# Routed attention into a SwiGLU layer: another order for the first head pair, zero matmuls between its assignments, and new steps for the preparation of pairs 2 to 6

## The chip, the cores and the metric

The kernel runs on one core of one Trainium2 chip. The metric is the device time of one execution in microseconds (us); the time of the kernel before is the median of three runs. Engine names are those of the profile: PE is TensorE's matmuls, PEld its weight loads, DVE is VectorE, ACT is ScalarE, POOL is GpSimd, SP is SyncE, which here only issues DMAs.

## The reference

Attention by clusters and then a feed-forward layer. Every query and key is assigned to the nearest of 16 centroids of its head, and a query attends only to keys of its own cluster.

```python
# q, k, v: 4 batches x 8 heads x 768 tokens x 64; centroids: 8 heads x 16 x 64
q_assign = argmax(einsum('bhsd,hcd->bhsc', q_n, c_n))      # k_assign alike
mask = q_assign[:, :, :, None] == k_assign[:, :, None, :]
scores = where(mask, matmul(q, k^T) / sqrt(64), -1e9)
attn = softmax(scores);  x = attn @ v                      # x: 3072 tokens x 512
xn = x / rms(x) * rms_g
out = (silu(xn @ w_gate) * (xn @ w_val)) @ w_out           # d_ff 1536
```

## The kernel before

Heads go in pairs: pair `pi` holds two heads of one batch, and there are 16 pairs, four to a batch. One head of one batch is a *slot* (32 of them). The mask is made part of the scores' matmul: for each head a tile `aug` of 80 rows holds 64 rows of q (or k) and 16 rows that are a one-hot code of the cluster, so that one matmul with a depth of 80 gives score and mask together. There are three sets of `aug` tiles, so pair 4 uses the set of pair 1.

**Steps.** The main loop goes through steps; a slot has 9 steps (`NCH`), and `at(step, fn)` hangs a piece of other work on a step. In the first 96 steps a score tile is *wide*: every third step four matmuls (L375) fill 128x1536 of PSUM, in three banks, and one ACT instruction takes the exponential of it (L378, `pT<-scw`). There are 32 such wide chunks, and chunk k belongs to steps 3(k-1) to 3k-1. Two wide tiles exist, so the matmuls of chunk k wait for the exponential of chunk k-2. In steps 2 to 7 of a slot `pv_group` multiplies the slot before with its values (L389), and in step 8 `pv_norm` normalises it on DVE (L398, L399). From step 96 on (`FFN0`) the feed-forward matmuls of the finished batch (L477, L510) run between narrower score tiles.

**Preparing a pair** (`prep_parts`) has 13 pieces, hung on steps in this order: T0 to T3 turn q and k of the two heads (three transposes on PE into one PSUM tile, L209, and a copy of 128x384 out of it, L213 on DVE or L215 on ACT); CAST writes the 64 rows of `aug` on POOL (L220); SP multiplies with the centroids (L233); TR, MX, CMP, SCL and BACK make the one-hot code on DVE (L240, L245, L250, L256, L261); PLACE sends its rows into `aug` by four DMAs (L272); CASTV turns v into bf16 on POOL (L225). The tiles of T0 to T3 and of SP all come from `ps_t`, a pool of one PSUM bank, so each waits until the one before has been read.

**Every engine works in the written order** (`manual_schedule`): nothing is reordered, and an instruction that waits holds all that are behind it on its engine.

**The first pair** can't be prepared ahead, and has code of its own: it makes the one-hot code by tokens (`assign0`, `pick0`) and brings it into rows by a matmul with an identity (`rows0`, `rows1`). `keep_warm` issues matmuls of zeros that nothing reads. A pool `ps_first` of six PSUM banks serves all of this, and is closed before the two wide tiles take its banks; the first turn of pair 1 is also in it. Where `t_tile` is called before that, it takes `ps_first`.

Of the kernel before, what the change touches and what calls it, by code (L numbers as in the profile page):

```python
# [8 lines left out]
F32 = mybir.dt.float32  # L9
# [4 lines left out]
PSUM = bass.MemoryType.PSUM  # L14
# [5 lines left out]
def kernel(  # L20
# [12 lines left out]
    nc = tc.nc  # L33
    B, H, S, D = q.shape
    NC = centroids.shape[1]
# [28 lines left out]


    first = ExitStack()
    ps_first = first.enter_context(tc.tile_pool(name="ps_first", bufs=6, space=PSUM))
    wide = ExitStack()
    WCH = 3
    late = {}  # L70
# [62 lines left out]

    def keep_warm(n, w_ps=None):
        if w_ps is None:
            w_ps = ps_first.tile([P, CH], F32, name="w_ps", tag="f")
        for _ in range(n):
            nc.tensor.matmul(w_ps, lhsT=zeros[:, 0:P], rhs=zeros, start=True, stop=True)  # L138
        return w_ps
# [19 lines left out]
    def put_centroids():  # L159
        c_ps = ps_t.tile([P, P], F32, name="c_ps", tag="t")  # L160
        nc.tensor.transpose(c_ps, c2[:, :, :].rearrange("p a d -> p (a d)"), ident_f)
        c_pv.append(c_ps[:, :].rearrange("p (h c) -> p h c", c=NC))
        nc.vector.tensor_copy(cbd[0:D, 0:2, :, 0], c_pv[0][0:D, 0:2, :])
        nc.scalar.copy(cbd[D:P, 0:2, :, 1], c_pv[0][D:P, 0:2, :])

    def rest_of_centroids():
        nc.vector.tensor_copy(cbd[0:D, 2:, :, 0], c_pv[0][0:D, 2:, :])
        nc.vector.tensor_copy(cbd[D:P, 2:, :, 1], c_pv[0][D:P, 2:, :])
# [17 lines left out]


    def t_tile(name):
        pool, tag = ps_t, "t"
        if "wide" not in late:  # L190
            pool, tag = ps_first, "f"
        return pool.tile([P, HS], F32, name=name, tag=tag)

    def prep_parts(pi):
        st = pi % NSET
# [3 lines left out]
        def t_group(g):  # L199
            a, side = divmod(g, 2)  # L200
            if qk32[0] is None:
                qk32[0] = prep.tile([P, 4, HS], F32, name="qk32", tag="qk32", bufs=3)
            if pi == 1 and g in (1, 3):
                tp = ps_pv.tile([P, HS], F32, name="tp", tag="acc")
            else:
                tp = t_tile("tp")
            src = loads[pi, side]
            for i in range(TH):
                nc.tensor.transpose(tp[:, i * P:(i + 1) * P], src[:, a, i * P:(i + 1) * P], ident_f)  # L209
            dst = qk32[0][:, g, :]  # L210
            on_dve = g > 0 if pi == 1 else pi < 7 or g % 2
            if on_dve:
                nc.vector.tensor_copy(dst, tp)  # L213
            else:
                nc.scalar.copy(dst, tp)  # L215
# [63 lines left out]
    as0 = {}  # L279
    oh0 = {}  # L280

    def turn0(g):
        tp = ps_first.tile([P, HS], F32, name="tp", tag="f")
        a, side = divmod(g, 2)
        for i in range(TH):
            nc.tensor.transpose(tp[:, i * P:(i + 1) * P], loads[0, side][:, a, i * P:(i + 1) * P], ident_f)  # L286
        if a:
            nc.vector.tensor_copy(qk0[:, g, :], tp)
        else:
            nc.scalar.copy(qk0[:, g, :], tp)  # L290

    def cast0(a):
        for side in range(2):
            for par in range(2):
                src = qk0[par * D:(par + 1) * D, 2 * a + side, :]
                dst = aug[0][a][0:D, side, par * HS:(par + 1) * HS]
                if a:
                    nc.gpsimd.tensor_copy(dst, src)
                else:
                    nc.scalar.copy(dst, src)  # L300

    def assign0(a, side):
        if a == 0:
            as0[a, side] = ps_first.tile([P, TH * 2 * NC], F32, name="as0", tag="f")
            dst = as0[a, side]
        else:
            if side == 0:
                as0[a] = ps_pv.tile([P, 2, TH * 2 * NC], F32, name="as1", tag="acc")
            dst = as0[a][:, side, :]
        for i in range(TH):  # L310
            nc.tensor.matmul(dst[:, i * 2 * NC:(i + 1) * 2 * NC], lhsT=qk0[:, 2 * a + side, i * P:(i + 1) * P],  # L311
                             rhs=cbd[:, a, :, :].rearrange("p c r -> p (c r)"), start=True, stop=True)

    def pick0(a, sides, src):
        n = len(sides) * TH
        view = src.rearrange("p (n c r) -> p n r c", c=NC, r=2)
        mx = small.tile([P, n, 2], F32, name="mx0", tag="mx0")
        nc.vector.tensor_reduce(mx, view, axis=AX, op=ALU.max)
        if a not in oh0:
            oh0[a] = const.tile([P, 2, TH * 2 * NC], BF16, name=f"oh0{a}")  # L320
        for j, side in enumerate(sides):
            nc.vector.tensor_tensor(oh0[a][:, side, :].rearrange("p (n c r) -> p n r c", c=NC, r=2),
                                    view[:, j * TH:(j + 1) * TH], mx[:, j * TH:(j + 1) * TH, :].unsqueeze(3)
                                    .to_broadcast([P, TH, 2, NC]), op=ALU.is_ge if side else ALU.is_lt)

    def rows0(side):
        o_ps = ps_first.tile([P, HS], F32, name="o_ps", tag="f")
        ov = oh0[0][:, side, :].rearrange("p (n c r) -> p n r c", c=NC, r=2)
        for i in range(TH):
            for r in range(2):  # L330
                nc.tensor.matmul(o_ps[32 * r:32 * r + NC, i * P:(i + 1) * P], lhsT=ov[:, i, r, :],
                                 rhs=(ident_n, ident_b)[side], start=True, stop=True, tile_position=(0, 32 * r))
        for r in range(2):
            dst = aug[0][0][D:KA, side, r * HS:(r + 1) * HS]
            if r:
                nc.vector.tensor_copy(dst, o_ps[32 * r:32 * r + NC, :])
            else:
                nc.scalar.copy(dst, o_ps[32 * r:32 * r + NC, :])

    def rows1():  # L340
        o_ps = ps_t.tile([P, HS], F32, name="o_ps", tag="t")
        for i in range(TH):
            for side in range(2):
                nc.tensor.matmul(o_ps[32 * side:32 * side + 32, i * P:(i + 1) * P],
                                 lhsT=oh0[1][:, side, i * 2 * NC:(i + 1) * 2 * NC],
                                 rhs=(ident_n, ident_b)[side], start=True, stop=True, tile_position=(0, 32 * side))
        o_sb = const.tile([64, HS], BF16, name="o_sb")
        nc.vector.tensor_copy(o_sb, o_ps[0:64, :])
        for side in range(2):
            nc.sync.dma_start(out=aug[0][1][D:KA, side, :].rearrange("c (r n) -> c r n", r=2),  # L350
                              in_=o_sb[32 * side:32 * side + 2 * NC, :])
# [192 lines left out]

    T0, T1, T2, T3, CAST, SP, TR, MX, CMP, SCL, BACK, PLACE, CASTV = range(13)
    p0, p1, p2, p3 = (prep_parts(pi) for pi in range(4))
    turn_w = keep_warm(7)
    turn0(0)
    turn0(1)
    turn0(2)  # L550
    put_centroids()
    turn0(3)
    keep_warm(2, turn_w)
    assign0(0, 0)
    assign0(0, 1)
    pick0(0, (0,), as0[0, 0][:, :])
    cast0(0)
    pick0(0, (1,), as0[0, 1][:, :])
    rows0(0)
    assign0(1, 0)  # L560
    rows0(1)
    assign0(1, 1)
    rest_of_centroids()
    pick0(1, (0, 1), as0[1][:, :, :].rearrange("p a n -> p (a n)"))
    cast0(1)
    p1[T0]()
    first.close()
    late["wide"] = wide.enter_context(tc.tile_pool(name="ps_wide", bufs=2, space=PSUM,
                                                 reuse_waits="tile"))
# [4 lines left out]
    for i, step in ((T1, 0), (T2, 3), (T3, 4), (CAST, 5), (SP, 6), (TR, 6), (MX, 7), (CMP, 8), (SCL, 9), (BACK, 10),  # L574
                    (PLACE, 10), (CASTV, 11)):
        at(step, p1[i])
    for i, step in ((T0, 10), (T1, 14), (T2, 16), (T3, 19), (CAST, 20), (SP, 21), (TR, 21), (MX, 22), (CMP, 23), (SCL, 24),
                    (BACK, 25), (PLACE, 25), (CASTV, 26)):
        at(step, p2[i])
    for i, step in ((T0, 24), (T1, 27), (T2, 29), (T3, 31), (SP, 33), (CAST, 33), (TR, 34), (MX, 35), (CMP, 36), (SCL, 37),  # L580
                    (BACK, 38), (PLACE, 38), (CASTV, 40)):
        at(step, p3[i])
    for pi in range(2, 4):
        at(10, lambda pi=pi: load_part(pi, 2))
# [21 lines left out]
    for pi in range(4, B * NP):  # L606
        base = 2 * NCH * (pi - 2) + {7: 14, 8: 10, 9: 4}.get(pi, 0)
        steps = (-11, -8, -5, -2, 0, 0, 2, 3, 4, 5, 6, 7, 10)
        if pi == 4:
            steps = (0, 2, 4, 7, 9, 9, 10, 12, 13, 14, 15, 16, 18)  # L610
        elif pi == 5:
            steps = (-6, -3, -1, 2, 4, 4, 5, 6, 7, 8, 9, 10, 12)
        elif pi == 6:
            steps = (-11, -8, -5, -2, 0, 0, 2, 3, 4, 4, 5, 6, 7)
        elif pi > 6:
            steps = (-8, -6, -4, -2, 0, 0, 2, 3, 4, 5, 6, 6, 10)
        for fn, step in zip(prep_parts(pi), steps):
            at(base + step, fn)
        if pi < B * NP - 3:
            at({6: 100, 7: 118}.get(pi, base + 12), lambda pi=pi: load_pair(pi + 3))  # L620
# [62 lines left out]
```

## Time and profile before

| | |
|---|---|
| time, median of three runs (lowest, highest) | 349.26 us (348.62, 350.96) |
| the profiled execution's own time; its span | 351.38 us; 349.6 us |
| PE busy, share of the span | 336.0 us, 96% |
| DVE busy, ACT busy, POOL busy | 223.4, 226.3 and 90.4 us |
| wide exponentials (L378, 128x1536) | 32, of 1456 ns in the mean |
| idle time of ACT before them | 13.4 us |
| narrow exponentials (L378, 128x512) | 192, of 598 ns |
| copies of T0 to T3 on DVE (L213, 128x384) | 41, of 551 ns |

The page lists busy time, then the span in 40 slices of 8.7 us with a digit for the busy tenths and one for the TensorE clock that was granted, then the costliest groups of instructions with the idle time of their engine before them and what ended it. A busy engine isn't an engine at its peak[...]. Other views answer for a stretch of time: the timeline (start, duration, engine, line, tiles, idle time before and what ended it), the chain that ended last, and busy time by windows.

### The profile page before, as it was taken

To read this page: it belongs to the slowest core of one execution; us is meant where nothing else is said; L and a number is where in the kernel's file an instruction comes from. 1 tells how busy PE (TensorE), PEld (TensorE's weight loads), DVE (VectorE), ACT (ScalarE), POOL (GpSimd) and SP (SyncE) were. 2 spreads that over 40 slices of the span, in tenths; PEclk is the share of its full clock that TensorE was granted. 3 is DMA by queue.
4 is the path that set the end of the run, shared out by engine and by line. 5 is a ranking of instruction groups with operands and counts; after the bars stand their busy time and mean duration, and the time that the engine had idled before them with its cause. 6 is when DMAs were issued, how large, how long until landed. Compare 5 with 4: busy or idle time off the path is not lost.

```text
span 349.6 us, 7568 instructions
## 1 busy us (share of the span) xinstructions
PE 336.0 (96%) x2948; PEld 208.8 (60%) x2980; DVE 223.4 (64%) x469; ACT 226.3 (65%) x391; POOL 90.4 (26%) x125
## 2 busy tenths in 40 slices
PE   8998888999999999999999999999999999999996
PEld 5655565676676566565656656566666655555554
DVE  3476678869676667776656468785545577756550
ACT  4487777998786677776767668687777434232322
POOL 4265689309531303141030214120000001000000
PEclk9699999999999999999999999999999999999999
DMA  7165899952944405145141001212000012200012
GB/s 260 64 217 173 194 278 222 261 163 50 248 90 139 158 29 182 53 36 194 33 146 43 2 36 39 47 57 62 33 1 32 30 50 58 77 30 30 33 60 90
DMA packets 36739, 34.94 MB, mean 100 GB/s; under 512 B 13520, under 2 KB 33632, under 8 KB 36704
## 3 DMA queue, kind: packets, MB, share of 16 engines
q1 hardware_dynamic: 30496, 29.44, 26.7%
q0 software_dynamic: 5920, 4.79, 9.1%
q8 instruction: 23, 0.38, 0.4%
q10 hardware_dynamic: 288, 0.23, 0.2%
q14 instruction: 12, 0.10, 0.1%
HBM read 28.61 MB, written 6.29 MB: 100 GB/s over the span
## 4 chain that ended last, share of the span: by engine, by line
PE 87%; DVE 5%; ACT 2%; DMA 2%; issue 1%; POOLq 0%; POOL 0%; DVEq 0%; ACTq 0%
PE gp L477 17%; PE vp L477 17%; PE dp L510 17%; PE sc L375 12%; PE acc L389 8%; PE tp L209 6%; PE scw L375 3%; PE sp L233 3%; DMA aug<-ohT 2%; ACT pT L378 2%; PE w_ps L138 1%; DVE qk L213 1%; PE as L311 1%; PE tp L286 1%; DVE ohT L261 1%
## 5 line engine op out<-in xcount | busy, mean ns | idle before, releaser
L378 ACT ACTIVATE pT<-sc 128x512 bf16<-128x512 f32 x192 | 113.7, 598 | 44.5 <-PE sc L375 44.1
L486 DVE SCALAR_TENSOR_TENSOR uu<-th,gp 128x384 f32<-128x384 f32 x96 | 53.0, 552 | 66.3 <-ACT th L482 66.2
L477 PE MATMUL vp<-xnT,wv 128*128 128x384 bf16 x384 | 78.1, 325 | 0.2 <-DVE gvT L492 0.2
L477 PE MATMUL gp<-xnT,wg 128*128 128x384 bf16 x384 | 78.1, 325 | 0.1
L389 PEld LDWEIGHTS <-pT 128*128 128x128 bf16 x1152 | 57.5, 97 | 30.2 <-issue 2.8
L482 ACT ACTIVATE th<-gp 128x384 f32<-128x384 f32 x96 | 47.2, 492 | 43.3 <-PE gp L477 40.6
L375 PE MATMUL sc<-aug 80*128 80x512 bf16 (+1 forms) x256 | 73.0, 327 | 0.0
L510 PE MATMUL dp<-wo,gvT 128*128 128x512 bf16 (+1 forms) x268 | 71.2, 369 | 1.6
L220 POOL CAST aug<-qk 64x768 bf16<-64x768 f32 x60 | 51.8, 863 | 64.7 <-DVE qk L213 46.9
L389 PE MATMUL acc<-vbf,pT 128*128 128x65 bf16 x1152 | 63.8, 194 | 1.5 <-DVE x L399 0.7
L492 DVE TENSOR_TENSOR gvT<-uu,vp 128x384 bf16<-128x384 f32 x96 | 52.6, 548 | 5.8 <-PE vp L477 0.8
L477 PEld LDWEIGHTS <-wg 128*128 128x128 bf16 x384 | 37.2, 97 | 30.1 <-issue 0.6
L378 ACT ACTIVATE pT<-scw 128x1536 bf16<-128x1536 f32 x32 | 45.7, 1456 | 13.4 <-PE scw L375 12.9
L477 PEld LDWEIGHTS <-wv 128*128 128x128 bf16 x384 | 37.1, 97 | 18.6 <-issue 0.5
L375 PEld LDWEIGHTS <-aug 80*128 80x128 bf16 x384 | 33.8, 99 | 17.3 <-issue 8.1
L510 PEld LDWEIGHTS <-gvT 128*128 128x128 bf16 x300 | 29.2, 98 | 24.3
L213 DVE COPY qk<-tp 128x384 f32<-128x384 f32 x41 | 22.5, 551 | 16.5 <-PE tp L209 16.4
L375 PE MATMUL scw<-aug 80*128 80x512 bf16 (+1 forms) x128 | 27.3, 337 | 0.7 <-ACT qk L215 0.6
L443 DVE SCALAR_TENSOR_TENSOR xn<-x,ir,g_b 128x512 bf16<-128x512 bf16 x24 | 20.3, 862 | 5.3 <-POOL ir L435 4.3
L225 POOL CAST vbf<-v_in 128x768 bf16<-128x768 f32 x16 | 13.5, 844 | 34.7 <-issue 34.3
L209 PE MATMUL tp<-ident_f,k_in 128*128 128x128 f32 x90 | 16.2, 291 | 2.7 <-DVE qk L213 2.7
L399 DVE TENSOR_TENSOR x<-acc,inv 128x384 bf16<-128x384 f32 x32 | 17.8, 557 | 1.1
(84 smaller groups left out, 206.6 us busy)
## 6 DMA issues: line engine op xcount, KB each, us to landing
v_in<-in_v_dram SPq DMA_DIRECT2D x16, 384.0 KB, 4.6
out_dram<-ob SPq DMA_DIRECT2D x23, 256.0 KB, 2.0
q_in<-in_q_dram SPq DMA_DIRECT2D x15, 384.0 KB, 4.6
k_in<-in_k_dram SPq DMA_DIRECT2D x15, 384.0 KB, 4.3
wg<-in_moe_w_gate_dram POOLq DMA_DIRECT2D x4, 384.0 KB, 8.1
wv<-in_moe_w_val_dram POOLq DMA_DIRECT2D x4, 384.0 KB, 7.9
wo<-in_moe_w_out_dram POOLq DMA_DIRECT2D x4, 384.0 KB, 7.3
aug<-ohT SPq DMA_DIRECT2D x57, 24.0 KB, 2.3
```

Of the source, the lines that this page charges most:

```text
L209: nc.tensor.transpose(tp[:, i * P:(i + 1) * P], src[:, a, i * P:(i + 1) * P], ident_f)
L213: nc.vector.tensor_copy(dst, tp)
L220: nc.gpsimd.tensor_copy(aug[st][a][0:D, :, par * HS:(par + 1) * HS], qk32[0][par * D:(par + 1) * D, 2 * a:2 * a + 2, :])
L375: nc.tensor.matmul(sc[:, o:o + n], lhsT=ag[:, 1, kc * P:(kc + 1) * P], rhs=ag[:, 0, qo:qo + n], start=True, stop=True)
L378: nc.scalar.activation(pts[slot][:, j * CH:(j + nch) * CH], sc[:, :nch * CH], ACT.Exp, scale=scale)
L389: nc.tensor.matmul(acc[:, TORD[g], :], lhsT=pts[slot][:, kc * S + g * P:kc * S + (g + 1) * P], rhs=vb[:, a, TORD[kc], :], start=(kc == 0), ...
L443: nc.vector.scalar_tensor_tensor(st["xn"][:, tl, :], x_t[b][:, t, :], st["ir", m][:, tl:tl + 1], g_b, op0=ALU.mult, op1=ALU.mult)
L477: nc.tensor.matmul(pt[:, :HS], lhsT=w[:, dc, fc * P:(fc + 1) * P], rhs=xnT[b, m][:, :, dc, :], start=(dc == 0), stop=(dc == DC - 1))
L482: nc.scalar.activation(th, pt[:, :HS], ACT.Tanh, scale=0.5)
L486: nc.vector.scalar_tensor_tensor(uu, th, 1.0, pt[:, :HS], op0=ALU.add, op1=ALU.mult)
L492: nc.vector.tensor_tensor(gvT[half][:, fc, :], uu, pt[:, :HS], op=ALU.mult)
L510: nc.tensor.matmul(dp, lhsT=gvT[hf][:, f, tl * P:(tl + 1) * P], rhs=wo[:, f, cols], start=(f == 0), stop=(f == FC - 1))
```

## The change

For the first pair: the six banks become two pools of three, `ps_fa` and `ps_fb`; the one-hot rows of `rows0` for the two halves go to a tile each, copied by ACT and DVE; nine zero matmuls stand at the front for seven, the two ahead of the assignments become one, one follows two of every three assignment matmuls, and one comes before the first score chunk; the zero matmuls write a tile of `ps_pv`. The third turn is copied by ACT, four more casts are ordered otherwise, two of them on POOL instead of ACT, and the rest of the centroids comes earlier on DVE. Pair 1's first turn is moved to `ps_t`, ahead of the last `pick0`.

For pairs 2 to 4 the copy of the third turn (T2) goes from DVE to ACT. Pairs 2 to 6 have new steps. All matmuls of the main loop, the feed-forward and all pairs from 7 on are as before.

```diff
-    ps_first = first.enter_context(tc.tile_pool(name="ps_first", bufs=6, space=PSUM))
+    ps_fa = first.enter_context(tc.tile_pool(name="ps_fa", bufs=3, space=PSUM))
+    ps_fb = first.enter_context(tc.tile_pool(name="ps_fb", bufs=3, space=PSUM))
...
     def keep_warm(n, w_ps=None):
         if w_ps is None:
-            w_ps = ps_first.tile([P, CH], F32, name="w_ps", tag="f")
+            w_ps = ps_pv.tile([P, CH], F32, name="w_ps", tag="acc")
...
-        nc.scalar.copy(cbd[D:P, 0:2, :, 1], c_pv[0][D:P, 0:2, :])
+        nc.vector.tensor_copy(cbd[D:P, 0:2, :, 1], c_pv[0][D:P, 0:2, :])
...
     def t_tile(name):
-        pool, tag = ps_t, "t"
-        if "wide" not in late:
-            pool, tag = ps_first, "f"
-        return pool.tile([P, HS], F32, name=name, tag=tag)
+        return ps_t.tile([P, HS], F32, name=name, tag="t")
...
-            if pi == 1 and g in (1, 3):
+            if pi == 1 and g == 2:
                 tp = ps_pv.tile([P, HS], F32, name="tp", tag="acc")
...
-            on_dve = g > 0 if pi == 1 else pi < 7 or g % 2
+            on_dve = g > 0 if pi == 1 else g != 2 if pi < 5 else pi < 7 or g % 2
...
-    def turn0(g):
-        tp = ps_first.tile([P, HS], F32, name="tp", tag="f")
+    def turn0(g, eng):
         a, side = divmod(g, 2)
+        tp = (ps_fb if a else ps_fa).tile([P, HS], F32, name="tp", tag="f")
...
-        if a:
-            nc.vector.tensor_copy(qk0[:, g, :], tp)
-        else:
-            nc.scalar.copy(qk0[:, g, :], tp)
-
-    def cast0(a):
-        for side in range(2):
-            for par in range(2):
...
+        eng(qk0[:, g, :], tp)
+
+    def cast0(a, side, eng):
+        for par in range(2):
+            eng(aug[0][a][0:D, side, par * HS:(par + 1) * HS], qk0[par * D:(par + 1) * D, 2 * a + side, :])
...
     def assign0(a, side):
         if a == 0:
-            as0[a, side] = ps_first.tile([P, TH * 2 * NC], F32, name="as0", tag="f")
+            as0[a, side] = ps_fb.tile([P, TH * 2 * NC], F32, name="as0", tag="f")
...
         for i in range(TH):
             nc.tensor.matmul(dst[:, i * 2 * NC:(i + 1) * 2 * NC], lhsT=qk0[:, 2 * a + side, i * P:(i + 1) * P],
                              rhs=cbd[:, a, :, :].rearrange("p c r -> p (c r)"), start=True, stop=True)
+            if i % 2 == 0:
+                keep_warm(1, w_ps)
...
     def rows0(side):
-        o_ps = ps_first.tile([P, HS], F32, name="o_ps", tag="f")
...
+        o_ps = [(ps_fb if side and r else ps_fa).tile([P, HS], F32, name="o_ps", tag="f") for r in range(2)]
...
     def rows1():
-        o_ps = ps_t.tile([P, HS], F32, name="o_ps", tag="t")
+        o_ps = ps_pv.tile([P, HS], F32, name="o_ps", tag="acc")
...
-    turn_w = keep_warm(7)
-    turn0(0)
-    turn0(1)
-    turn0(2)
+    by_act, by_dve, by_pool = nc.scalar.copy, nc.vector.tensor_copy, nc.gpsimd.tensor_copy
+    w_ps = keep_warm(9)
+    turn0(0, by_act)
+    turn0(1, by_act)
     put_centroids()
-    turn0(3)
-    keep_warm(2, turn_w)
+    cast0(0, 1, by_pool)
+    cast0(0, 0, by_act)
+    turn0(2, by_act)
+    turn0(3, by_dve)
+    keep_warm(1, w_ps)
     assign0(0, 0)
     assign0(0, 1)
+    rest_of_centroids()
     pick0(0, (0,), as0[0, 0][:, :])
-    cast0(0)
+    cast0(1, 0, by_pool)
+    cast0(1, 1, by_pool)
     pick0(0, (1,), as0[0, 1][:, :])
     rows0(0)
     assign0(1, 0)
     rows0(1)
     assign0(1, 1)
-    rest_of_centroids()
+    p1[T0]()
     pick0(1, (0, 1), as0[1][:, :, :].rearrange("p a n -> p (a n)"))
-    cast0(1)
-    p1[T0]()
+    keep_warm(1, w_ps)
     first.close()
...
-    for i, step in ((T0, 10), (T1, 14), (T2, 16), (T3, 19), (CAST, 20), (SP, 21), (TR, 21), (MX, 22), (CMP, 23), (SCL, 24),
+    for i, step in ((T0, 12), (T1, 15), (T2, 17), (T3, 19), (CAST, 20), (SP, 21), (TR, 22), (MX, 23), (CMP, 23), (SCL, 24),
                     (BACK, 25), (PLACE, 25), (CASTV, 26)):
         at(step, p2[i])
-    for i, step in ((T0, 24), (T1, 27), (T2, 29), (T3, 31), (SP, 33), (CAST, 33), (TR, 34), (MX, 35), (CMP, 36), (SCL, 37),
-                    (BACK, 38), (PLACE, 38), (CASTV, 40)):
+    for i, step in ((T0, 27), (T1, 29), (T2, 31), (T3, 33), (SP, 35), (CAST, 35), (TR, 36), (MX, 37), (CMP, 38), (SCL, 39),
+                    (BACK, 39), (PLACE, 39), (CASTV, 41)):
         at(step, p3[i])
...
         if pi == 4:
-            steps = (0, 2, 4, 7, 9, 9, 10, 12, 13, 14, 15, 16, 18)
+            steps = (4, 6, 9, 11, 12, 12, 13, 14, 15, 16, 16, 17, 18)
         elif pi == 5:
-            steps = (-6, -3, -1, 2, 4, 4, 5, 6, 7, 8, 9, 10, 12)
+            steps = (0, 2, 4, 6, 7, 7, 7, 8, 9, 10, 10, 11, 12)
         elif pi == 6:
-            steps = (-11, -8, -5, -2, 0, 0, 2, 3, 4, 4, 5, 6, 7)
+            steps = (-8, -6, -3, 0, 2, 2, 4, 5, 6, 6, 7, 8, 9)
```

The steps of pairs 4, 5 and 6 count from 36, 54 and 72.

More of the change, by code (lines that the diff above doesn't have):

```diff
@@ L280 @@
     oh0 = {}
-    def turn0(g):
-        tp = ps_first.tile([P, HS], F32, name="tp", tag="f")
+    def turn0(g, eng):
         a, side = divmod(g, 2)
+        tp = (ps_fb if a else ps_fa).tile([P, HS], F32, name="tp", tag="f")
         for i in range(TH):
             nc.tensor.transpose(tp[:, i * P:(i + 1) * P], loads[0, side][:, a, i * P:(i + 1) * P], ident_f)
-        if a:
-            nc.vector.tensor_copy(qk0[:, g, :], tp)
-        else:
-            nc.scalar.copy(qk0[:, g, :], tp)
-    def cast0(a):
-        for side in range(2):
-            for par in range(2):
[L295 to L300, printed above, removed]
+        eng(qk0[:, g, :], tp)
+    def cast0(a, side, eng):
+        for par in range(2):
+            eng(aug[0][a][0:D, side, par * HS:(par + 1) * HS], qk0[par * D:(par + 1) * D, 2 * a + side, :])
     def assign0(a, side):
         if a == 0:
-            as0[a, side] = ps_first.tile([P, TH * 2 * NC], F32, name="as0", tag="f")
+            as0[a, side] = ps_fb.tile([P, TH * 2 * NC], F32, name="as0", tag="f")
             dst = as0[a, side]
@@ L307, in assign0 @@
             if side == 0:
-                as0[a] = ps_pv.tile([P, 2, TH * 2 * NC], F32, name="as1", tag="acc")
+                as0[a] = ps_fb.tile([P, 2, TH * 2 * NC], F32, name="as1", tag="f")
             dst = as0[a][:, side, :]
@@ L326, in rows0 @@
     def rows0(side):
-        o_ps = ps_first.tile([P, HS], F32, name="o_ps", tag="f")
         ov = oh0[0][:, side, :].rearrange("p (n c r) -> p n r c", c=NC, r=2)
+        o_ps = [(ps_fb if side and r else ps_fa).tile([P, HS], F32, name="o_ps", tag="f") for r in range(2)]
         for i in range(TH):
             for r in range(2):
-                nc.tensor.matmul(o_ps[32 * r:32 * r + NC, i * P:(i + 1) * P], lhsT=ov[:, i, r, :],
+                nc.tensor.matmul(o_ps[r][32 * r:32 * r + NC, i * P:(i + 1) * P], lhsT=ov[:, i, r, :],
                                  rhs=(ident_n, ident_b)[side], start=True, stop=True, tile_position=(0, 32 * r))
[L333 to L338, printed above, removed]
+        for r, eng in enumerate((nc.scalar.copy, nc.vector.tensor_copy)):
+            eng(aug[0][0][D:KA, side, r * HS:(r + 1) * HS], o_ps[r][32 * r:32 * r + NC, :])
     def rows1():
-        o_ps = ps_t.tile([P, HS], F32, name="o_ps", tag="t")
+        o_ps = ps_pv.tile([P, HS], F32, name="o_ps", tag="acc")
         for i in range(TH):
```

## The prediction

> **What bounds the kernel now.** I read the page first, then busy time by windows, the chain, and the timeline of ACT beside that of PE and DVE.
>
> ```profile
> PE   8998888999999999999999999999999999999996
> PEclk9699999999999999999999999999999999999999
> L378 ACT ACTIVATE pT<-scw 128x1536 bf16<-128x1536 f32 x32 | 45.7, 1456 | 13.4 <-PE scw L375 12.9
> ```
>
> PE is full only from the eighth slice on, and the granted clock dips in the second. The wide exponentials last 45.7 us and ACT was idle 13.4 us ahead of them, nearly all for scores. Windows part the two regimes, and show the dip (columns: stretch, length, busy PE, PEld, DVE, ACT, POOL, granted clock, DMA share, GB/s):
>
> ```profile
> 30.00:40.00 10.00, 7.68 (x89) 4.99 (x88) 7.07 (x17) 6.12 (x5) 4.86 (x6) 1.00 0.52 141
> 80.00:90.00 10.00, 10.00 (x102) 6.48 (x95) 9.35 (x19) 7.93 (x17) 8.21 (x10) 1.00 0.52 90
> 9.00:10.00 1.00, 1.00 (x14) 0.85 (x16) 0.65 (x3) 0.80 (x2) 0.92 (x2) 1.00 0.96 358
> 11.00:12.00 1.00, 1.00 (x6) 0.86 (x6) 0.94 (x4) 0.00 (x0) 0.00 (x0) 0.50 0.00 0
> 17.00:18.00 1.00, 1.00 (x8) 0.85 (x7) 0.65 (x2) 1.00 (x1) 0.83 (x1) 0.78 0.40 55
> ```
>
> From about 72 us PE is the bound, with the same matmuls in both kernels. So the change is worth what it shifts the end of the 32 wide chunks, one for one. Ahead of that no engine is full: the chunks wait on a chain through PE, one PSUM bank and DVE. The clock was at half from about 10.7 to 17.5 us, and the chain shows the price:
>
> ```profile
> 1.18 3.17 PE w_ps L138 x7
> 4.34 1.98 PE tp L286 x9
> 7.68 1.26 PE as L311 x12
> 10.32 1.11 PE as L311 x6
> 12.69 1.44 PE scw L375 x4
> 23.04 0.65 PE scw L375 x4
> 33.72 0.36 PE tp L209 x3
> ```
>
> Seven zero matmuls in 3.17 us (0.43 to 0.45 each) and turns of 0.22 are the slow rate too, though the clock reads 1.00 there: before its first record it says nothing. An assignment pass costs 0.105 full and 0.185 slow, a chunk 0.65 and 1.44, a turn of three 0.36 and some 0.66.
>
> The stalls later on look like this (start, duration, then idle time before it):
>
> ```profile
> 37.70 0.59 DVE L250 TENSOR_TENSOR oh<-tr,mx 128x384 bf16<-128x384 f32 x1
> 38.18 0.55 DVE L213 COPY qk<-tp 128x384 f32<-128x384 f32 x1
> 38.78 0.55 PE L209 MATMUL tp<-ident_f,k_in 128*128 128x128 f32 x3 [1.16 <-DVE qk L213]
> 39.17 0.81 PE L375 MATMUL scw<-aug 80*128 80x512 bf16 x4
> 40.02 4.45 ACT L378 ACTIVATE pT<-scw 128x1536 bf16<-128x1536 f32 x3 [1.65 <-PE scw L375]
> 10.86 0.55 DVE L336 CAST aug<-o_ps 16x384 bf16<-16x384 f32 x1 [0.45 <-ACT aug L338]
> ```
>
> A turn waits for the one `ps_t` bank, its copy stands behind the one-hot work of the pair before, the next chunk stands behind the turn, and ACT loses 1.65 us. The last line is the first pair's one shared bank: DVE waits for ACT.
>
> [...]
>
> **The change, the first 19 us.** Nine zero matmuls at 0.43 from 1.18 end at 5.02, where seven ended near 4.2; q was there at 4.14, so the turns start 0.85 later. Twelve turns and the centroids at 0.213 end at 7.7 (before: 7.2). Then on PE at full rate: zero 0.21, the first head's assignments 1.26 plus four zeros 0.85, rows 0.32, assignments 0.63 plus 0.42, rows 0.3, again 1.05, pair 1's turn 0.37, zero 0.21: 5.6 us, so the first chunk starts at 13.3 against 12.69. The picks keep up: DVE copies the fourth turn to 8.5, `rest_of_centroids` (2 x 0.26) to 9.05, picks to 9.6 and 10.45; the rows are wanted at 10.0 and 11.4. POOL's six casts of 0.55 end near 11, v's at 11.8; both are wanted after 17. The separate banks take 0.45 off evacuations that PE's queue covers: nothing. That the ACT copy of pair 1's turn no longer holds a wide bank removes the 0.55 wait at 12.69, already in the sum. So at a full clock the first exponential starts at 14.2, as before (14.17). The gain follows: chunks at 0.65 and turns at 0.37 give exponentials at 14.2, 15.7, 17.1 and 18.8, where before they stood at 14.17, 16.71, 18.45 and 20.06. **-1.3 us** at chunk 4; there SP's wait for the last copy and the rows' DMA (issued 15.1 and 15.7, landing in 1.9) set it.
>
> That zeros hold the clock is unmeasured.[...] I take full clock; the other end is the cold rival.
>
> **Pairs 2 to 6.** I walked PE, DVE and ACT in the new order with these durations: chunk 0.65 and 0.25 more to its exponential, exponential 1.44, turn 0.37, copy 0.55 beginning 0.57 after its turn starts, L389 group 0.185, SP 0.83, one-hot DVE work 0.58+0.56+0.6+0.26+0.58, `pv_norm` 0.75. Exponential starts, before (timeline; second of a merged group 1.45 on) and worked out:
>
> ```
> chunk    4     7     11    13    17    19    22    24    26
> before  20.06 25.2  33.39 36.92 44.75 49.37 54.05 58.89 62.05
> after   18.8  23.9  31.2  36.1  43.7  47.2  54.2  59.7  63.8
> ```
>
> - Chunk 7: T2 of pair 2 waits at 22.4 for T1's copy; the placed rows land at 23.0. Idle 0.8.
> - Chunk 11: T1 of pair 3 waits until 29.97 for T0's copy, which stands behind BACK (to 28.6) and `pv_norm`. Idle 1.2; 1.62 before.
> - Chunks 13 and 17: the new thing. T2's copy on ACT stands behind the running exponential of 1.44, and T3 needs its bank. For pair 3 the copy ends at 33.2, T3 goes at 33.2, its copy ends at 34.35, SP takes until 35.2: idle 1.5. For pair 4 T2 and T3 share chunk 16: idle 1.3. Each copy also takes 0.48 of ACT itself, 1.44 in all. On DVE the same copies were 3 x 0.55 off the path.
> - Chunk 20 (T1 behind `pv_norm` and T0's copy): 1.2. Chunk 22 (SP behind T3's copy): 1.4.
> - Chunk 24: pair 5's one-hot work is pushed into steps 61 to 64, and T0's copy of pair 6 is behind all of it and a sum of squares: T1 waits to 58.0. Idle 2.3; 1.11 before. Chunk 26: 1.3.
>
> From 7 to 26 that is 39.9 us against 36.85: **+3.1 us**. With the -1.3 this is +1.8. Not in it: 52.9 and 55.3 us saw two DVE operations of 0.6 take 1.19 and 1.17 (the timeline); in the new order the second delays T0's copy too, 0 to 1 us. Each of the seven stalls may be off by 0.4 either way, some 2.5 us if they go together.
>
> Costed at nothing: the order of g_b and pair 3's PLACE on SP (one issue of 0.58; the rows are wanted at chunk 19, eight us later), the two POOL instructions that change places (pair 4's casts are wanted at chunk 25), the moved loads of weights (same steps). If the cover went, each costs its 0.6 to 1.7.
>
> **The sum.** Profiled execution: 351.38 + 1.8 = 353.2. It lies 2.1 above the median, 349.26, and I can't tell how much of that is the profiler and how much a long cold stretch that other runs draw shorter (their spread is 2.3). If all is the profiler, the new median is 351.1; if all is the cold, it is 353.2, since the change always buys that part. I take 352.0. Under 1% (3.5 us) is about what a measurement of this kernel can't tell from no change.
>
> **Rivals.**
> 1. *The spacing works (not slower).* DVE loses three copies and the pairs' work overlaps less, so the 10.2 us of idle from chunk 4 to 26 shrinks instead of growing. For it: DVE was busy 7 to 8 of 10 us here and most stalls name its copy. Against: T3 behind an ACT copy. It decides if T2's copy is ready before the exponential ahead of it has started. Half of the way from my +3.1 to -5 is -1; with -1.3: 347.0.
> 2. *The clock still falls.* Then from 10.7 the zeros cost 0.43: assignments, rows, turn, zero and chunk take some 2.9 longer, the next chunks 1 to 1.5 more, so chunk 4 is at 22.9: +2.8, and +3.1 after. About 355.2.[...]
> 3. *Front only:* the middle is equal, 349.26 - 1.3 = 348.0; within rival 1.
>
> **Chances.** Forecast 0.52 (349.5 to 354.5, two fifths of it beyond 352.75), rivals 1 and 3 0.28 (two fifths below 345.8), rival 2 0.20 (nine tenths beyond 352.75). Slower 0.21 + 0.18 = 0.39, faster 0.12, same 0.49. The range reaches 346.5 to 355.5.
>
> **What would show it.** Right: no half clock after 8 us; first wide exponential near 14.2, the fourth near 18.8; exponentials 13 and 17 idle over 1 us, with T3 waiting for an ACT copy; the 26th 1 to 3 us later than 62.05; the stretch after 75 us unchanged in length. Wrong: the 26th at 60 or earlier, copies on ACT that nobody waits for, or a clock at half past 10 us.

## The result: slower, and the profile after

Changed kernel: 359.06 us median of 4 runs (358.04 to 360.52); before, on the same chip: 349.27 us (348.62 to 350.96). Ratio of the two 1.0276, with a 95% interval of [1.0225, 1.0326]. The profiled execution took 359.07 us with a span of 357.3 us, against 351.38 and 349.6. Runs of one kernel differ in how long the clock was recorded at half, so where I part them by the mean clock recorded for each run, I say so.

The page of the changed kernel, the same three lines as before (PE busy in tenths of each of 40 slices of 8.9 us, granted clock, the wide exponentials: busy time and mean, then the idle time ahead):

```profile
PE   8997886989999999999999999999999999999996
PEclk9998988799999999999999999999999999999999
L365 ACT ACTIVATE pT<-scw 128x1536 bf16<-128x1536 f32 x32 | 45.0, 1452 | 20.0 <-PE scw L362 19.7
```

The dip in the second slice is gone, and three new ones stand in the fourth, sixth and seventh to eighth. ACT now waits 20.0 us ahead of the wide exponentials, where it waited 13.4: 6.6 of the 7.7 us that the span grew. Windows of the changed kernel (columns as in the prediction) show the front, one of the dips, and a stretch in which PE is the bound:

```profile
11.00:12.00 1.00, 1.00 (x10) 0.90 (x10) 0.66 (x2) 0.37 (x1) 0.29 (x1) 1.00 0.02 9
28.00:29.00 1.00, 0.00 (x0) 0.00 (x0) 0.97 (x4) 0.94 (x1) 0.00 (x0) 1.00 0.07 19
29.00:30.00 1.00, 0.86 (x10) 0.72 (x11) 0.43 (x1) 0.00 (x0) 0.00 (x0) 0.99 0.09 25
30.00:31.00 1.00, 1.00 (x5) 0.46 (x3) 0.56 (x1) 0.00 (x0) 0.31 (x1) 0.50 0.17 48
31.00:32.00 1.00, 1.00 (x15) 0.96 (x14) 0.00 (x0) 0.72 (x1) 0.94 (x2) 0.50 0.09 25
80.00:90.00 10.00, 10.00 (x104) 6.80 (x103) 8.45 (x19) 7.99 (x17) 3.52 (x5) 1.00 0.01 2
```

At 11 us the clock is full now (0.50 before). PE does nothing at all from 28 to 29 us, and a microsecond after it is back at work its clock is 0.50. The clock records give half from 29.98 to 33.39, 50.46 to 53.87 and 60.70 to 67.52 us, 13.65 us or four times 3.41 (each 3.41 us is called a window here); before, it was two windows, 10.62 to 17.44. From 75 us on PE is as full as it was.

Two places of the timeline (start, duration, idle time before). First, the hole at 28 us:

```profile
26.11 0.83 POOL L223 CAST vbf<-v_in 128x768 bf16<-128x768 f32 x1
26.26 1.13 DVE L248 TENSOR_TENSOR oh<-tr,mx 128x384 bf16<-128x384 f32 x1
27.71 0.58 DVE L259 STREAM_TRANSPOSE ohT<-oh 128x384 bf16<-128x384 bf16 x1
28.40 0.56 DVE L386 TENSOR_TENSOR x<-acc,inv 128x384 bf16<-128x384 f32 x1
28.88 0.55 DVE L211 COPY qk<-tp 128x384 f32<-128x384 f32 x1
29.11 0.34 PE L376 MATMUL acc<-vbf,pT 128*128 128x65 bf16 x6 [1.65 <-DVE x L386]
29.48 0.55 PE L207 MATMUL tp<-ident_f,k_in 128*128 128x128 f32 x3
29.87 1.37 PE L362 MATMUL scw<-aug 80*128 80x512 bf16 x4
31.28 1.45 ACT L365 ACTIVATE pT<-scw 128x1536 bf16<-128x1536 f32 x1 [2.34 <-PE scw L362]
```

PE waits 1.65 us for `pv_norm` (L386), which stands on DVE behind the one-hot work of pair 2. T1 of pair 3 then waits for T0's copy (28.88), and the chunk behind it goes at half clock: its first four matmuls take 1.37 where they take 0.81 at full. The same place in the prediction had 1.2 us of idle ahead of this exponential; it was 2.34. Second, the longest stall:

```profile
60.47 0.52 DVE L211 COPY qk<-tp 128x384 f32<-128x384 f32 x1
61.04 0.90 PE L207 MATMUL tp<-ident_f,k_in 128*128 128x128 f32 x3 [2.45 <-DVE qk L211]
62.41 1.47 PE L362 MATMUL scw<-aug 80*128 80x512 bf16 x4
63.92 1.45 ACT L365 ACTIVATE pT<-scw 128x1536 bf16<-128x1536 f32 x1 [4.03 <-PE scw L362]
```

T1 of pair 6 waits for T0's copy behind the one-hot work of pair 5. PE idles 2.45 us; the clock falls at 60.70; the turn and the chunk then go at half, and chunk 24 comes 4.03 us late instead of 2.3.

The exponentials of the prediction's table, measured in the changed kernel:

```
chunk     4     7     11    13    17    19    22    24    26
forecast 18.8  23.9  31.2  36.1  43.7  47.2  54.2  59.7  63.8
measured 17.70 22.95 31.28 36.77 44.22 47.6  56.87 63.92 69.45
```

(19 is the second of a group that starts at 46.31, and some 1.3 later.) Up to chunk 19 the forecast holds within 1.1 us; of the 5.65 us that chunk 26 is later than forecast, 5.25 appear between chunks 19 and 26.

### The profile page after: what moved, and what is told of

It reads as the page before. It is cut to its first block, busy times and chain, and to the rows that moved or that the text cites. A ratio compares the mean times of both kernels' runs of the same rounds, so it can differ in the third digit from the quotient of the medians.

```text
span 357.3 us, 7594 instructions
## 1 busy us (share of the span) xinstructions
PE 339.7 (95%) x2957; PEld 211.7 (59%) x2990; DVE 223.2 (62%) x466; ACT 226.1 (63%) x392; POOL 90.6 (25%) x127
## 4 chain that ended last, share of the span: by engine, by line
PE 87%; DVE 8%; issue 2%; DMA 0%; ACT 0%; POOL 0%; POOLq 0%; ACTq 0%; DVEq 0%
PE gp L464 17%; PE vp L464 17%; PE dp L497 16%; PE sc L362 12%; PE acc L376 9%; PE tp L207 6%; PE scw L362 4%; PE sp L231 3%; PE w_ps L139 2%; DVE qk L211 1%; DVE oh L248 1%; DVE xn L430 1%; DVE tr L238 1%; DVE mx L243 1%; PE as L300 1%
## 5 line engine op out<-in xcount | busy, mean ns | idle before, releaser
L376 PEld LDWEIGHTS <-pT 128*128 128x128 bf16 x1152 | 60.2, 100 | 31.8 <-issue 4.2
L376 PE MATMUL acc<-vbf,pT 128*128 128x65 bf16 x1152 | 65.9, 197 | 3.9 <-DVE x L386 3.7
L211 DVE COPY qk<-tp 128x384 f32<-128x384 f32 x38 | 20.9, 553 | 25.4 <-PE tp L207 25.3
L362 PE MATMUL scw<-aug 80*128 80x512 bf16 (+1 forms) x128 | 29.1, 354 | 0.3 <-DMA v_in<-in_v_dram 0.2
L223 POOL CAST vbf<-v_in 128x768 bf16<-128x768 f32 x16 | 13.4, 837 | 33.7 <-issue 33.2
L386 DVE TENSOR_TENSOR x<-acc,inv 128x384 bf16<-128x384 f32 x32 | 17.8, 558 | 1.1
```

Of the source, the lines that this page charges most:

```text
L362: nc.tensor.matmul(sc[:, o:o + n], lhsT=ag[:, 1, kc * P:(kc + 1) * P], rhs=ag[:, 0, qo:qo + n], start=True, stop=True)
L376: nc.tensor.matmul(acc[:, TORD[g], :], lhsT=pts[slot][:, kc * S + g * P:kc * S + (g + 1) * P], rhs=vb[:, a, TORD[kc], :], start=(kc == 0), ...
```

## The experiments

Two theories stood after this. *Clock*: the new stalls drop the clock, and the half rate is most of what was missed. *Waits*: the stalls themselves, above all T3 behind T2's copy on ACT, are longer than I worked out, and the dips only accompany them. All ratios are to the kernel before, run beside the experiment on the same chip. e1 to e4 share one chip, e5 to e8 a second, e9 to e11 a third, and e12 has a fourth. The runs of before that kept the full clock have medians of 348.58, 348.08, 348.80 and 348.32 us on these four, so a difference of less than 0.7 us between experiments on two chips shows nothing.

**e1, the new front alone.** The changed kernel with the old steps and the old copies:

```diff
-            on_dve = g > 0 if pi == 1 else g != 2 if pi < 5 else pi < 7 or g % 2
+            on_dve = g > 0 if pi == 1 else pi < 7 or g % 2
...
-            steps = (-8, -6, -3, 0, 2, 2, 4, 5, 6, 6, 7, 8, 9)
+            steps = (-11, -8, -5, -2, 0, 0, 2, 3, 4, 4, 5, 6, 7)
```

> The first pair as changed, pairs 2 to 6 as before (old steps, T2 copied on DVE). Theory: the front is a gain of its own, exponential 4 near 17.7 instead of 20.06, and the loss is all in pairs 2 to 6: time 347.0 us, 2.3 under before. Rival: the pairs' chain gives the front's gain back, because their stalls are set by DVE and not by when the first chunk starts: 349 us, with exponential 26 near 62.

348.67 us (347.62 to 350.69, 20 runs), ratio 0.9968 [0.9947, 0.999]. Span 346.4, full clock in all 20 runs. That is 1.1 us under before on this chip (349.78), where the theory had 2.3. The rival's account is not right either: in the profile exponential 26 starts at 58.72, not near 62. The front's whole worth is that the clock no longer falls: 12 of the 39 runs of the kernel before on this chip stayed at full clock by themselves, and their median is 348.58. Against those the new front brings nothing.

**e2, pairs 2 to 6 alone.** The kernel before with the new steps and T2's copies on ACT:

```diff
-            on_dve = g > 0 if pi == 1 else pi < 7 or g % 2
+            on_dve = g > 0 if pi == 1 else g != 2 if pi < 5 else pi < 7 or g % 2
...
-            steps = (-11, -8, -5, -2, 0, 0, 2, 3, 4, 4, 5, 6, 7)
+            steps = (-8, -6, -3, 0, 2, 2, 4, 5, 6, 6, 7, 8, 9)
```

> The first pair as before, pairs 2 to 6 as changed (new steps, T2 of pairs 2 to 4 on ACT). Theory: the two parts add, so this is the change without the front's 2.3 us: about 361 us, with half clock in the middle. Rival: the stalls of the change come from a front that runs ahead of the pairs' preparation; then this is near before, 350 to 352 us.

359.88 us (358.28 to 362.67, 4 runs), ratio 1.0296 [1.0207, 1.0385]. All of the loss is here; front and pairs add up within the intervals.

**e3, the changed kernel with T2's copies back on DVE; e4, the changed kernel with the old steps and T2's copies on ACT.** These part the two edits inside the pairs.

```diff
 # e3
-            on_dve = g > 0 if pi == 1 else g != 2 if pi < 5 else pi < 7 or g % 2
+            on_dve = g > 0 if pi == 1 else pi < 7 or g % 2
 # e4
-    for i, step in ((T0, 27), (T1, 29), (T2, 31), (T3, 33), (SP, 35), (CAST, 35), (TR, 36), (MX, 37), (CMP, 38), (SCL, 39),
+    for i, step in ((T0, 24), (T1, 27), (T2, 29), (T3, 31), (SP, 33), (CAST, 33), (TR, 34), (MX, 35), (CMP, 36), (SCL, 37),
...
-            steps = (-8, -6, -3, 0, 2, 2, 4, 5, 6, 6, 7, 8, 9)
+            steps = (-11, -8, -5, -2, 0, 0, 2, 3, 4, 4, 5, 6, 7)
```

> The change with T2 of pairs 2 to 4 copied on DVE again. Theory of the prediction (ACT copies behind an exponential make the new stalls): 1.4 us of ACT work and two stalls of 1.3 go, and some of the half clock with them: 353 to 355 us. Rival (the new steps make the stalls, at T1 behind the one-hot work): within 1.5 us of the change, 358 to 360 us.

> The change with pairs 2 to 6 at the steps of before, T2 of pairs 2 to 4 still copied on ACT. Theory of the prediction: the two or three stalls behind ACT copies stay, 351 to 354 us. Rival (the steps make the stalls): near the first pair alone plus 1.4 us of ACT, 347 to 349 us, without half clock in the middle.

e3: 356.31 us (354.56 to 356.52, 4 runs), ratio 1.0184 [1.0126, 1.0242]. e4: 349.21 us (348.37 to 350.94, 20 runs), ratio 0.9988 [0.9971, 1.0005], at full clock in every run. With the old steps the copies on ACT cost 0.54 us (e4 less e1, same chip). The timeline of e4 shows why:

```profile
22.44 0.47 ACT L213 COPY qk<-tp 128x384 f32<-128x384 f32 x1
22.96 0.55 PE L207 MATMUL tp<-ident_f,k_in 128*128 128x128 f32 x3 [0.42 <-ACT qk L213]
```

A turn does wait for the copy on ACT, but 0.42 us, not more than a microsecond. Most of the cost comes with the new steps. e3 gains 2.75 us on the changed kernel, and lies between its two expected ranges. Its profiled run, the fastest of the four, recorded a mean clock of 0.990, the changed kernel's 0.981: at 3.41 us for a window that stands for two windows at half instead of four. The mean clock of the other three (0.985) stands for three windows, one fewer. So e3 alone can't say whether the copy or the clock was saved.

**e5, the clock taken apart from the waits.** The changed kernel with 24 more zero matmuls, put in the three places where PE stood idle. They write the wide tile of the next chunk before its scores do; no wait is taken away and no step moved. (The timeline lacks the record of one zero matmul in each place.)

```diff
+    ahead = {}
+
+    def fill(step, n):
+        sc = late["wide"].tile([P, WCH * CH], F32, name="scw", tag="scw")
+        keep_warm(n, sc[:, 0:CH])
+        ahead[step] = sc
...
+    for step, n in ((28, 8), (55, 6), (66, 10)):
+        extra.setdefault(step, []).insert(0, lambda step=step, n=n: fill(step // WCH * WCH + WCH, n))
```

> The change with 24 more zero matmuls, in three stalls: 8, 6 and 10 of them are written into the wide tile of the next chunk (which is free) just ahead of the turns that wait at steps 29, 56 and 66. No wait is removed; only PE's idle time is filled. Theory (the stalls themselves were foreseen within 1 to 3 us in all, and the missed term is the half clock that each long stall brings): no half clock in the middle, 353 to 355 us. Rival (the stalls are simply longer than worked out, the clock is a side effect): 357 to 360 us, with a full clock.

353.42 us (352.92 to 353.79, 7 runs), ratio 1.0097 [1.0066, 1.0128]: 5.6 us faster than the changed kernel, for work that computes nothing. The chips don't make this difference: between chunks 7 and 26 of the two profiles it is the same, 46.50 against 40.86 us. Page and timeline of e5:

```profile
PEclk9999999999999999999999999999999999999999
L374 ACT ACTIVATE pT<-scw 128x1536 bf16<-128x1536 f32 x32 | 45.0, 1452 | 14.6 <-PE scw L371 14.3
```

```profile
27.15 1.89 PE L139 MATMUL scw<-zeros 128*128 128x512 bf16 x7 [0.19 <-ACT pT L374]
30.27 1.45 ACT L374 ACTIVATE pT<-scw 128x1536 bf16<-128x1536 f32 x1 [1.83 <-PE scw L371]
41.26 0.55 PE L207 MATMUL tp<-ident_f,k_in 128*128 128x128 f32 x3 [1.03 <-ACT qk L213]
42.50 1.45 ACT L374 ACTIVATE pT<-scw 128x1536 bf16<-128x1536 f32 x1 [1.29 <-PE scw L371]
55.09 2.32 PE L139 MATMUL scw<-zeros 128*128 128x512 bf16 x9
59.31 2.89 ACT L374 ACTIVATE pT<-scw 128x1536 bf16<-128x1536 f32 x2 [2.75 <-PE scw L371]
```

The clock is full throughout; the idle time of ACT falls from 20.0 to 14.6. Before chunk 11 it is 1.83 instead of 2.34, before chunk 24 2.75 instead of 4.03. The *clock* theory holds for 5.6 us of the loss. *Waits* keeps the rest: at full clock e5 is still 4.75 us above e1, or 5.25 if each is taken against the full-clock runs of before on its own chip. Whatever the zeros themselves cost is in that.

**e6, pairs 4 to 6 at their old steps; e8, pair 6 alone at its old steps** (both on the changed kernel):

```diff
 # e6
-            steps = (4, 6, 9, 11, 12, 12, 13, 14, 15, 16, 16, 17, 18)
+            steps = (0, 2, 4, 7, 9, 9, 10, 12, 13, 14, 15, 16, 18)
...
-            steps = (0, 2, 4, 6, 7, 7, 7, 8, 9, 10, 10, 11, 12)
+            steps = (-6, -3, -1, 2, 4, 4, 5, 6, 7, 8, 9, 10, 12)
...
 # e6 and e8
-            steps = (-8, -6, -3, 0, 2, 2, 4, 5, 6, 6, 7, 8, 9)
+            steps = (-11, -8, -5, -2, 0, 0, 2, 3, 4, 4, 5, 6, 7)
```

> The change with pairs 4, 5 and 6 at their old steps; pairs 2 and 3 at the new ones. If the loss is mostly pair 6's T1 behind pair 5's one-hot work (idle 4.0 ahead of exponential 24) and what follows from it: 351 to 353 us. If pairs 2 and 3 carry it alike (idle 2.3 ahead of exponential 11, half clock from 30 us): 354 to 356 us.

> The change with pair 6 alone at its old steps, so that T0 is ordered at step 61, ahead of pair 5's SCL and BACK. If exponential 24's idle of 4.0 and the half clock after it come from T0's copy behind that work: 4 to 6 us under the change, 353 to 355 us. If another wait takes its place: 357 to 359 us.

e6: 350.39 us (348.14 to 354.13, 12 runs), ratio 1.0016 [0.9979, 1.0053]; five of its runs kept the full clock, median 348.46, seven recorded 0.989 to 0.995, median 351.25. e8: 355.70 us (355.39 to 359.01, 4 runs), ratio 1.0195 [1.0114, 1.0277], with two dips of one window each in the profile (a mean clock of 0.83 in the ten us from 30 and in those from 50); it saves 3.4 us, less than the 4 to 6 of its theory. At full clock, then, most of e5's loss is in the new steps of pairs 4 to 6: 5.0 us by the medians (353.42 less 348.46), 3.4 against the slowest of e6's five (350.00, the profiled one). Those of pairs 2 and 3 cost little at full clock, but with them the clock fell in seven of twelve runs, and with the old ones in none of forty (e1 and e4).

**e7, e9 and e10, what the zeros between the assignments are worth.** e7 is e1 without the zeros between assignments, e9 is e1 with two of the eight, e10 is e7 with seven zeros at the start instead of nine.

```diff
 # e7
-            if i % 2 == 0:
-                keep_warm(1, w_ps)
 # e9
-            if i % 2 == 0:
+            if i == 0 and not side:
 # e10, on e7
-    w_ps = keep_warm(9)
+    w_ps = keep_warm(7)
```

> The changed first pair with the old steps and DVE copies (as in the run of the front alone), without the eight zero matmuls between the assignments; the other zeros stay. If these hold the clock: half clock for 3.4 to 6.8 us after 9 us in most runs, 350 to 351 us against 348.7. If the clock holds without them, it is 1 us shorter than with them: 347.5 us.

> The changed first pair with old steps and DVE copies, with two zero matmuls in place of the eight between the assignments (after the first matmul of q's assignments of each head). Theory: a zero costs its 0.21 us on PE's path and its worth is only that the clock holds. If two are enough to hold it in all runs: 347.9 to 348.1 us, no run at half clock. If not: the median is 348 us, with some runs 1.4 to 2.8 us longer, as without any.

> The changed first pair with old steps and DVE copies, no zero matmuls between the assignments, and seven at the front instead of nine. The turns can start 0.85 us sooner. If the front's zeros set the start: 347.1 us. If the two more are needed to lift the clock early (the turns then run at the slow rate): 347.9 us or more, with half clock in more runs.

e7: 347.86 us (346.9 to 351.25, 20 runs), ratio 0.9954 [0.993, 0.9977]. e9: 348.29 us (347.16 to 351.05, 16 runs), 0.9951 [0.9926, 0.9975]. e10: 348.22 us (347.13 to 352.76, 22 runs), 0.9965 [0.9942, 0.9989]. With the eight zeros the clock stayed full in 40 of 40 runs (e1 and e4); with two of them in 13 of 16, without them in 17 of 20 (e7) and, with seven at the start, in 15 of 22 (e10); in the kernel before in 44 of 132, over all four chips. So it is the rest of the new front that mostly holds the clock; the zeros close the last cases, and neither two of them (e9) nor seven at the start (e10) are enough. What they cost at full clock isn't settled, since the kernels ran on three chips: the full-clock median less that of before on the same chip is +0.1 us for e1, -0.3 for e7, -0.9 for e9 and -0.7 for e10, so 0.4 to 1.0. The three runs of e7 that lost the clock have a median of 350.18, 2.4 above its others; three runs in twenty at 2.4 are 0.36 us. So the zeros cost at least about as much as they insure. All three kernels beat the changed one, and the kernel before by half a per cent or less; the three can't be told apart by their intervals.

**e11, e5 with T2's copies on DVE; e12, e5 with pair 6 at its old steps** (and with the first two of the three fills). These size the copy and pair 6 at full clock.

```diff
 # e11
-            on_dve = g > 0 if pi == 1 else g != 2 if pi < 5 else pi < 7 or g % 2
+            on_dve = g > 0 if pi == 1 else pi < 7 or g % 2
 # e12
-    for step, n in ((28, 8), (55, 6), (66, 10)):
+    for step, n in ((28, 8), (55, 6)):
...
-            steps = (-8, -6, -3, 0, 2, 2, 4, 5, 6, 6, 7, 8, 9)
+            steps = (-11, -8, -5, -2, 0, 0, 2, 3, 4, 4, 5, 6, 7)
```

> The change with the 24 zero matmuls in three stalls and T2 of pairs 2 to 4 copied on DVE: what the copies on ACT cost among the new steps at a full clock. The prediction's walk has 1.4 us of ACT work and two stalls of 1.3 and 1.5 in them: 349.5 to 351 us against 353.4. Rival (as at the old steps, they cost half a microsecond, since DVE is what PE waits for): 352.5 to 353.5 us.

> The change with the first two of the three fills (8 and 6 zero matmuls) and pair 6 at its old steps: the share of pair 6 at a full clock, against 353.4 us with all three fills. Theory: T0's copy then stands ahead of pair 5's SCL and BACK, the 2.75 us of idle ahead of exponential 24 fall to about 1, and 351.5 to 352 us are left; the rest of the 5 us that pairs 4 to 6 lose is in pair 5's late T1 and SP. Rival: another wait takes the place, 353 to 353.5 us.

e11: 352.10 us (351.3 to 352.72, 19 runs), ratio 1.0056 [1.0039, 1.0074]. e12: 352.32 us (352.21 to 352.48, 4 runs), ratio 1.0095 [1.0068, 1.0123]. Against e5 that is 1.3 us for the copy and 1.1 for pair 6, on different chips. Each taken against the full-clock runs of before on its own chip, it is 2.0 and 1.3; in the profiles, from the first exponential to chunk 26 (50.58 us in e5, 49.20 in e11, 50.00 in e12), 1.4 and 0.6. So I take 1.3 to 2.0 and 0.6 to 1.3. The copy's share lies between the two expected ranges of e11. The timeline of e11 at chunks 13 and 17, where e5 had 1.60 ahead of the first, and 1.03 and 1.29 at the second:

```profile
35.70 4.14 ACT L374 ACTIVATE pT<-scw 128x1536 bf16<-128x1536 f32 x3 [1.41 <-PE scw L371]
40.91 0.55 PE L207 MATMUL tp<-ident_f,k_in 128*128 128x128 f32 x3
42.15 1.45 ACT L374 ACTIVATE pT<-scw 128x1536 bf16<-128x1536 f32 x1 [0.70 <-PE scw L371]
```

T3 no longer waits, and still chunk 17 is 0.70 us late. Of the 1.60 at chunk 13, 1.41 stay. In e12 the idle time ahead of chunk 24 falls from 2.75 to 1.70, but that ahead of chunk 22 grows from 1.41 to 2.56:

```profile
54.81 1.45 ACT L374 ACTIVATE pT<-scw 128x1536 bf16<-128x1536 f32 x1 [2.56 <-PE scw L371]
59.71 2.89 ACT L374 ACTIVATE pT<-scw 128x1536 bf16<-128x1536 f32 x2 [1.70 <-PE scw L371]
```

So another wait takes much of the place of pair 6's, and the time lies between the two expected ranges of e12. What stays of e5's loss, some 2 to 3 us, I put down to the new steps of pairs 4 and 5; no run has these alone.

## Why the prediction was wrong, step by step

It gave 352.0 us and a range to 355.5; the kernel takes 359.06. It had slower at 0.39, behind no difference at 0.49, and its range reached to 6.2 of the 9.8 us. Its steps in turn:

- **The clock beyond the front: the step that failed.** "I take full clock" was an assumption that no trace had shown, it was asked of the front only, and rival 2 let the clock fall only there. The seven stalls worked out for pairs 2 to 6 were priced as lost time of ACT, and never as gaps on PE with which the clock might fall. With three of them came four windows at half clock: 5.6 us, by e5, of the 7.06 us by which 352.0 was missed. The last section gives the busy time of PE in these places.
- **The walk through pairs 2 to 6: right in its places, short in its sum.** With the clock held by e5, idle ahead of chunks 11, 13, 17, 20, 22, 24 and 26 is 1.83, 1.60, 1.29, 1.72, 1.41, 2.75 and 1.11 us; the walk had 1.2, 1.5, 1.3, 1.2, 1.4, 2.3 and 1.3. From chunk 7 to 26 e5 takes 40.9 us (22.45 to 63.31), the walk 39.9. So +3.1 against before's 36.85 should have been +4.0. By medians it is +4.75 to +5.25 (e5 against e1). The largest errors are at chunks 11, 20 and 24, all three where T0's copy stands behind `pv_norm` and the one-hot work.
- **"The new thing", T2's copy on ACT: right at one chunk of two, and not the main cause.** I gave it 1.5 and 1.3 us at chunks 13 and 17. At chunk 17 the wait is there, 1.03 us in e5. At chunk 13 T3 waits only some 0.2 us for ACT in e5 (turns wait for ACT twice there, 1.2 us in all), and most of the idle time stays with the copies on DVE (1.41 of 1.60 us, e11). In all the copies cost 0.54 us with the old steps (e4), and 1.3 to 2.0 with the new ones (e11). The steps carry the rest. In the old ones, T0 of each of the pairs 3 to 6 was ordered one to three steps ahead of BACK of the pair before; in the new ones it comes in the same step or up to two after it. So T0's copy now stands behind the whole one-hot work on DVE, and T1 waits for the one `ps_t` bank. That is read from the order and the timelines; e6 agrees with it, and e12 shows that putting back pair 6 alone moves much of the wait to chunk 22.
- **The front: right in its mechanism, and near in its size.** No half clock after 8 us, first exponential at 13.24 (forecast 14.2; the slow rate ended at 6.08 us, where before it ended at 7.20), chunk 4 at 17.70 for 20.06: -2.36 on the profiles where I had -1.3. Some of that is luck: in the profiles with this front the first exponential starts anywhere from 12.73 (e5) to 13.75 (e11). By medians e1 is 1.1 us below before on its chip, but nothing below those runs of it that kept the clock. The open question of the sum, how much of the profiled 351.38 was a long cold stretch that other runs draw shorter, is answered by the 132 runs of before beside the experiments, parted by their mean clock: 348.53 with no window lost, 349.64 with one, 350.98 with two, so some 1.2 us for each. The profiled execution lost two, so the cold stretch is most of it.
- **The bottleneck reading: right.** Chunk 26 moved from 62.05 to 69.45, by 7.4 us, and the span by 7.7: what the wide chunks lose, the end loses. So it is in e1: chunk 26 comes 3.3 us earlier than in the kernel before, and the span is 3.2 shorter.
- **DVE operations of 1.19 us, left out of the sum at 0 to 1:** the compare at 26.26 above takes 1.13, and the cast of POOL at 26.11 lies beside it; the one at 37.19 takes 1.00 beside a cast at 36.91. The two slow compares in the kernel before (0.73 us at 28.99 and 1.19 at 52.90) lie beside casts that start at 28.45 and 52.82. In these four places the compare starts after the cast and takes 0.73 to 1.19 us; the other eight of the two profiles up to 75 us take 0.57 to 0.59. It wasn't tried with the cast moved away, so that the cast is the cause is not shown. At 26.26 it lengthens by 0.5 us the very chain that ends in the hole of 28 us.

The ledger by medians: front -0.6 (e1 less the 349.27 of the first comparison), steps and copies at full clock +4.75 (e5 less e1), lost clock +5.6 (changed kernel less e5). The three are links of one chain, so it is no check that they add up to the measured 9.8. By the ratios to before on the same chip they are -1.1, +4.5 and +6.3.

## What to carry to other kernels

Price a stall on PE twice: once as the time that its waiter loses, and again for the clock: here gaps of 1.5 to 2.5 us came with one or two windows at half, at about 1.4 us each (5.6 us for four). One profile at full clock doesn't show that the clock will hold: that of e6 is at full clock, and seven of its twelve runs were not. To see whether a dip in the clock is a cause or a companion, put zero matmuls in the gap and take no wait away; if the time falls, as it did by 5.6 us in e5, it was a cause. And when turns share one bank, the room between them must hold the turn and whatever stands on DVE ahead of its copy (at pair 6 of the changed kernel T1 waits until 61.04 for a copy that starts at 60.47): look there before blaming the engine to which a copy was moved.

## What was not expected of the hardware

Short gaps on PE came with a fall of the clock. The gaps ahead of the three dips were 1.65 us (27.45 to 29.11), 1.51 us (47.6 to 49.12) and 2.45 us (58.6 to 61.04); after the one of 1.02 us that ends at 42.98 in the same profile, and after those of 1.16 and 1.07 us that end at 38.78 and 48.08 in the kernel before, the clock stayed at 1.00. All changes of the clock within each of the two profiles lie a multiple of 3.41 us apart. Some windows of the changed kernel, laid on the times at which its clock changed:

```
window (us)      PE busy (us)  clock in it  clock in the next
26.56 to 29.98   1.74          full         half
40.22 to 43.63   2.15          full         full
47.04 to 50.46   1.81          full         half
57.28 to 60.70   1.19          full         half
60.70 to 64.11   3.07          half         half
64.11 to 67.52   3.37          half         full
```

From 12 to 72 us of this profile the three full-clock windows that were followed by half clock had 1.19 to 1.81 us of busy PE, as the profile has it, and the other full-clock windows 2.15 or more. In the kernel before the full-clock windows from 17.44 to 72 us had 2.35 or more, and none was followed by half clock. The third gap runs 0.34 us over the edge at 60.70; the window behind that edge had 3.07 us of busy PE, and the next one was at half too. What decides on the clock is not shown by this: in the kernel before PE was busy for the whole window from 7.20 to 10.62, mostly with narrow matmuls (128x32), and still the clock fell. With zeros in the three gaps (e5) the clock reads 1.00 throughout, and PE was busy for 4.75, 4.65 and 4.65 us of the five from 25, from 45 and from 55 us.
